# Asking earlier for an expert's first weights, and reordering the first batch's loads, in an attention and mixture-of-experts kernel

## The chip, the cores and the metric

The kernel runs on one core of a Trainium2 chip. The metric is the device time in microseconds (us) of one execution; the median of several runs counts.

## The reference

Sliding-window attention (window 128, a linear bias per head) is followed by a dense mixture of experts. All eight experts work on all tokens; a routing matrix, balanced by eight rounds of row and column normalisation, weighs their outputs.

```python
# q, k, v: (8 batches, 8 heads, 576, 64)
scores = q @ k.T / sqrt(64) + slope[h] * -abs(i - j)   # where 0 <= i - j < 128
attn = softmax(scores) @ v
x = attn.transpose(0, 2, 1, 3).reshape(4608, 512)
P = exp(x @ w_gate - max)
for _ in range(8):
    P /= P.sum(1) + 1e-9; P /= P.sum(0) + 1e-9; P *= N / E
out = sum(P[:, e:e+1] * (relu(x @ w1[e]) @ w2[e]) for e in range(8))   # w1: 512 x 1024, w2: 1024 x 512
```

## The kernel before

**Attention.** Each batch's 576 tokens are four blocks of 128 and a tail of 64. A step of the main loop is (b, kb, u): batch, key block, half of the heads (four). It makes the scores on PE (`scores`, tile psS), their exp on ACT (`exps`, tile pt), the mask product on DVE (`masks`), the product with v on PE (`values`, tile psN), and on DVE the reciprocal and the scaled result xsb. `turn_x` transposes a finished block into xT, the layout that the experts need. Scores, exp and mask of the next step are issued ahead of the values of this one.

**Loads of q and k.** For batch 0 they come in eight pieces on SP's DMA queue (`load_first`, L364), in pairs j = 0 to 3; ACT and DVE cast them to half precision (`cast_qk`), PE turns them (`turn_pe`, tile psT), ACT and DVE copy them to kN and qN. The 64 tail rows of q and k come in one tile t (`load_tail`, L290). They are turned on PE in one piece (`turn_pe` with j = 4), placed ahead of the values of block 2, and copied by ACT to tT; the scores of blocks 3 and 4 read tT. The v blocks (`load_v`, L410) are cast to half precision on POOL (`cast_v`, L423). Tiles of v and t share five buffers (tag s32), so the fifth load of v waits for the cast of the first.

**Weights.** `load_weights` asks for W1 (L100) and W2 (L102) of an expert. These are DMAs of POOL's queue, because they cast from 32 to 16 bits. Their place in POOL's program is the moment of the request: before, W1 of expert 0 stands behind the cast of v0 and ahead of the cast of v1; W2 stands behind two casts of the second half of batch 1's q (L315), which wait for its load (L301).

**The experts in the gaps.** Experts 0 and 1 run during the attention. A `Filler` holds units (expert, first block, number of blocks). A unit has layer-1 pieces (four matmuls into psh, then a relu by ACT or DVE into hT) and layer-2 pieces (matmuls hT by W2 into psy). `take` issues one piece. A unit may start when its blocks are below `filler.ready`. Layer-2 pieces are held back up to step 12 (`filler.hold`). The first two units are (expert 0, blocks 0 and 1) and (expert 0, blocks 2 and 3), with eight layer-1 pieces each, four matmuls of 256 columns per piece.

**Spins.** In the first 42 us PE also runs matmuls on a constant tile (`spin`, `spin_alone`), whose results nobody reads: three ahead of each half-block's values of batch 0, and some alone.

**Order.** The schedule is manual: each engine runs its instructions in the order in which the program issues them, and waits by semaphores. SP's DMAs use eight semaphores in turn, so each waits for the landing of the one eight before. The mask's columns for the tail are made by POOL in `tail_masks`, from columns that ACT's exps (`make_mask`) have written.

Behind the attention come the balancing, and experts 2 to 7 with Strassen's seven products in groups of 256 tokens (L983, L1080); they take some 650 us and the change does not touch them.

Of the kernel before, what the change touches and what calls it, by code (L numbers as in the profile page):

```python
# [9 lines left out]
FP16 = mybir.dt.float16  # L10
# [4 lines left out]
def kernel(  # L15
# [236 lines left out]
    if True:  # L252
# [4 lines left out]
        def make_mask(ys):  # L257
            for y in ys:
                nc.scalar.activation(
                    out=mask[:, y, P : 3 * P], in_=rel, func=AF.Exp, scale=-float(slopes[head_of[y]])  # L260
                )

        def tail_masks():

            nc.gpsimd.memset(mask[TL:P, :, 0:TL], 0.0)
            nc.gpsimd.tensor_copy(out=mask[0:TL, :, 0:TL], in_=mask[0:TL, :, P : P + TL])
            nc.gpsimd.tensor_copy(out=mask[:, :, TL:P], in_=mask[:, :, 2 * P : 2 * P + TL])

# [18 lines left out]
        def load_tail(b):  # L287
            t32 = asb.tile([P, H, Dh], FP32, name=f"t32_{b}", tag="s32", bufs=5)
            for lo, src in ((0, q), (TL, k)):
                nc.sync.dma_start(  # L290
                    out=t32[lo : lo + TL], in_=src[b, :, SM:S, :].rearrange("h s d -> s h d")
                )
            tails[b] = t32

        def load_qk(b, parts=1):
            q32 = per.tile([P, H, RI * Dh], FP32, name=f"q32_{b}", tag="a8", bufs=8)
            k32 = per.tile([P, H, RI * Dh], FP32, name=f"k32_{b}", tag="a8", bufs=8)
            w = H // parts
            for n in range(parts):
                for t, src in ((q32, q), (k32, k)):  # L300
                    nc.sync.dma_start(  # L301
                        out=t[:, n * w : n * w + w],
                        in_=src[b, n * w : n * w + w, 0:SM, :].rearrange("h (p i) d -> p h (i d)", i=RI),
                    )
            raw[b] = (q32, k32)
# [52 lines left out]
        def load_first():  # L358
            q32 = per.tile([P, H, RI * Dh], FP32, name="q32_0", tag="a8", bufs=8)
            k32 = per.tile([P, H, RI * Dh], FP32, name="k32_0", tag="a8", bufs=8)  # L360
            raw[0] = (q32, k32)
            for j in range(NDT):
                for n in (1, 0):
                    nc.sync.dma_start(  # L364
                        out=raw[0][n][:, 2 * j : 2 * j + 2, :],
                        in_=(q, k)[n][0, 2 * j : 2 * j + 2, 0:SM, :].rearrange(
                            "h (p i) d -> p h (i d)", i=RI
                        ),
                    )
            load_v(0)  # L370
            load_v(1)
            load_tail(0)
            load_v(2)
            load_v(3)
            load_v(4)
            homes(0)

        def turn_pe(b, kq, j):
# [27 lines left out]
        def load_v(m):  # L406
            b, kb = divmod(m, NKB)
            v32 = asb.tile([P, H, Dh], FP32, name=f"v32_{b}_{kb}", tag="s32", bufs=5)
            nk = P if kb < NKB - 1 else TL
            nc.sync.dma_start(  # L410
                out=v32[0:nk],
                in_=v[b, :, P * kb : P * kb + nk, :].rearrange("h s d -> s h d"),
            )
            v32s[b, kb] = v32

        def cast_v(m):
            b, kb = divmod(m, NKB)
            vt = asb.tile([P, H, Dh + 2], FP16, name=f"v_{b}_{kb}", tag="v", bufs=6)
            nk = P if kb < NKB - 1 else TL
            if nk < P:  # L420
                nc.gpsimd.memset(vt[nk:P], 0.0)
            nc.gpsimd.memset(vt[0:nk, :, Dh : Dh + 2], 1.0)
            nc.gpsimd.tensor_copy(out=vt[0:nk, :, 0:Dh], in_=v32s.pop((b, kb))[0:nk])  # L423
            vs[b, kb] = vt
# [35 lines left out]
        def exps(b, kb, u):  # L460
            ps = pss.pop((b, kb, u))
            pt = asb.tile([P, 4, 2 * P], FP16, name=f"pt_{b}_{kb}_{u}", tag="pt", bufs=4)
            nc.scalar.activation(out=pt, in_=ps.rearrange("p a y n -> p (a y) n"), func=AF.Exp, scale=scale)  # L463
            pts[b, kb, u] = pt
# [7 lines left out]
        def values(b, kb, u):  # L472

            nk = sizes(kb)
            if u == 0:
                xsbs[b, kb] = asb.tile([P, H, Dh], FP16, name=f"xsb_{b}_{kb}", tag="xsb", bufs=XSB)
            psN = aps.tile([P, GT], FP32, name=f"psN_{b}_{kb}_{u}", tag="pmm", bufs=4)
            if b == 0:
                spin(psN, 3)
            psN = psN[:, 0 : 4 * Dh + 4].rearrange("p (h d) -> p h d", h=4)  # L480
            ops = []
            for y in range(2):
                for hb in range(2):
                    hh = 2 * y + hb
                    if kb > 0:
                        t, at = (pts[b, kb - 1, u], P) if kb < NKB - 1 else (pts[b, kb - 1, u], TL)
                        ops.append((hh, t[:, 2 * hb + y, at : at + P], vs[b, kb - 1][:, 4 * u + hh, 0 : Dh + 1]))
                    t, at = (pts[b, kb, u], P * (kb == NKB - 2)) if kb < NKB - 1 else (pts[b, kb - 1, u], 0)
                    ops.append((hh, t[:, 2 * hb + y, at : at + P], vs[b, kb][:, 4 * u + hh, 0 : Dh + 1]))
            for i, (hh, lhsT, rhs) in enumerate(ops):  # L490
                nc.tensor.matmul(  # L491
                    out=psN[:, hh, :],
                    lhsT=lhsT,
                    rhs=rhs,
                    start=(i == 0),
                    stop=(i == len(ops) - 1),
                )
            if kb > 0:
                pts.pop((b, kb - 1, u))
            rden = asb.tile([P, 4], FP32, name=f"rden_{b}_{kb}_{u}", tag="rden", bufs=2)  # L500
            nc.vector.reciprocal(out=rden[0:nk, :], in_=psN[0:nk, :, Dh])
            nc.vector.tensor_tensor(
                out=xsbs[b, kb][0:nk, 4 * u : 4 * u + 4, :],
                in0=psN[0:nk, :, 0:Dh],
                in1=rden[0:nk, :].unsqueeze(2).to_broadcast([nk, 4, Dh]),
                op=ALU.mult,
            )
# [172 lines left out]
        load_first()  # L680
        spin_alone(20)
        make_mask(range(4))
        load_qk(1, 2)
        load_v(NKB)
        load_tail(1)
        cast_v(0)
        load_weights(0, 0, 1)
        cast_v(1)


        steps = [(b, kb, u) for b in range(B) for kb in range(NKB) for u in range(2)]
        for j in range(2):
            cast_qk(0, j)
            make_mask((4 + 2 * j, 5 + 2 * j))
            if j:
                spin_alone(4)
            turn_pe(0, 1, j)
            turn_pe(0, 0, j)
        tail_masks()
        cast_v(2)  # L700
        nc.gpsimd.dma_start(out=wg_sb, in_=moe_w_gate.rearrange("(dt p) e -> p dt e", p=P))
        cast_v(3)
# [2 lines left out]
            cast_qk(1, j, (0,), True)  # L705
        load_weights(0, 1, 2)
        cast_qk(0, 2)
        cast_qk(0, 3)
        spin_alone(4)
        scores(*steps[0])  # L710
        exps(*steps[0])
        spin_alone(4)
        turn_pe(0, 1, 2)
        turn_pe(0, 0, 2)
# [3 lines left out]
        for n, (b, kb, u) in enumerate(steps):  # L718
# [6 lines left out]
            if nxt:  # L725
                if nxt[0] < XPE and nxt[1:] == (RI - 2, 1):
                    turn_pe(nxt[0], 0, NDT)
                if nxt == (1, 0, 0):
                    filler.ready = RI
                    spin_alone(6)  # L730
                    for _ in range(NFT):
                        filler.take()
                    cast_qk(1, 0)
                    cast_qk(1, 1)
                    for j in range(NDT):
                        turn_pe(1, 1, j)
                        turn_pe(1, 0, j)
                        if j < 2:
                            cast_qk(1, j + 2, (1,))
                        filler.take()  # L740
                if nxt == (2, 0, 0):
                    filler.fill(8.5)
                    cast_qk(2, 0)
                    cast_qk(2, 1)
                    filler.fill(2.5)
                    for j in range(NDT):
                        turn_pe(2, 1, j)
                        turn_pe(2, 0, j)
                        if j < 2:
                            cast_qk(2, j + 2, (1,))  # L750
                        filler.fill(1.0)
                if n == 0:
                    scores(*nxt)
                elif nxt[2] == 0 and nxt[1] < NKB - 1:
                    scores(*nxt)
                    scores(*nxt[:2], 1)
                if nxt[1] < NKB - 1:
                    exps(*nxt)
            if nxt and nxt[1] < NKB - 1:
                masks(*nxt)  # L760
            got = filler.fill(1.0) if b else 0.0
            if (b, kb, u) == (1, 1, 0):
                spin_alone(8)
            values(b, kb, u)
# [572 lines left out]
```

## Time and profile before

| What | Value |
|---|---|
| runs shown | 990.17 us median of 3 (990.02 to 992.47) |
| the profiled execution | 995.15 us, its span 993.3 us |
| PE busy | 978.8 us (99%) |
| DVE, ACT, POOL busy | 692.2, 625.8, 210.5 us |
| PE busy, 0 to 10 us, 10 to 20, 20 to 30 | 6.07, 8.43, 8.61 us |
| PE busy, 30 to 40, 40 to 50, 50 to 60 | 9.17, 8.73, 9.90 us |
| W1 of expert 0 asked for, landed | 13.07, 25.15 us |
| W2 of expert 0 asked for, landed | 31.51, 43.20 us |
| first layer-1 and first layer-2 matmul on PE | 27.28, 43.25 us |

All times within the execution are from the start of its span. Parts of the page that matter here: the busy shares, the queues (q1 is the queue of SP's DMAs, q0 that of POOL's) and the chain that ended last. A landing is the moment at which a DMA's semaphore has its full count.

### The profile page before, as it was taken

Reading aid. Unit: us, or ns where it says so; the run is one execution under the profiler, and the core shown is the slowest. Engines: PE = TensorE matmul, PEld = TensorE weight load, DVE = VectorE, ACT = ScalarE, POOL = GpSimd, SP = SyncE. Lnnn points to the kernel's source line nnn. Section 1 sums busy time; section 2 is a strip of 40 time slices with the busy share of each in tenths; the row PEclk is TensorE's granted clock in tenths of the full one; section 3 lists DMA queues with packets and bytes.
Section 4 is the critical chain, followed back from the end, with each engine's and each line's share of the span. In section 5 each row is a group of like instructions: output and inputs, shape, how many; then the busy total and the mean of one; then the engine's idle time right before and its main releaser. Section 6 shows DMA issues by size and latency. Waiting matters only on the chain.

```text
span 993.3 us, 19600 instructions
## 1 busy us (share of the span) xinstructions
PE 978.8 (99%) x7247; PEld 627.0 (63%) x7247; DVE 692.2 (70%) x1546; ACT 625.8 (63%) x1000; POOL 210.5 (21%) x442
## 2 busy tenths in 40 slices
PE   7999999999999999999999999999999999999998
PEld 5655655565544566666666666666666666666665
DVE  5746766665588878767767676676676676676666
ACT  6645454555343657676776776777677676776774
POOL 3315353545110011111111111111211111111111
PEclk9999999999999999999999999999999999999999
DMA  9998999999999576656667656757756666665666
GB/s 212 237 262 191 211 228 220 221 193 181 229 195 188 92 134 137 128 123 133 129 123 133 146 119 130 147 120 125 144 117 123 143 128 124 141 131 124 142 116 124
DMA packets 383455, 155.03 MB, mean 156 GB/s; under 512 B 335296, under 2 KB 372928, under 8 KB 383360
## 3 DMA queue, kind: packets, MB, share of 16 engines
q1 hardware_dynamic: 359680, 110.87, 56.1%
q0 software_dynamic: 23248, 42.75, 19.8%
q8 instruction: 57, 0.93, 0.4%
q14 instruction: 38, 0.31, 0.1%
q10 hardware_dynamic: 432, 0.16, 0.1%
HBM read 77.25 MB, written 23.59 MB: 102 GB/s over the span
## 4 chain that ended last, share of the span: by engine, by line
PE 90%; DMA 5%; DVE 2%; SPq 1%; issue 1%; ACT 0%; POOL 0%; DVEq 0%; POOLq 0%
PE psM L1080 32%; PE psB L983 14%; PE psy L159 11%; PE psA L983 9%; PE psC L983 9%; PE psh L137 8%; PE psh L118 3%; DMA q<-in_q_dram 1%; PE psN L491 1%; PE psS L457 1%; DMA w2t<-in_moe_w_dram 1%; DMA ysp<-yo 1%; DMA v<-in_v_dram 1%; DMA hs<-s5y 0%; DVE pt L468 0%
## 5 line engine op out<-in xcount | busy, mean ns | idle before, releaser
L1080 PEld LDWEIGHTS <-hs 128*128 128x128 f16 x2996 | 292.6, 98 | 122.7 <-DVE hs L1051 0.8
L983 PEld LDWEIGHTS <-xset 128*128 128x128 f16 x1484 | 144.9, 98 | 91.2 <-issue 0.9
L1051 DVE TENSOR_TENSOR hs<-hs 128x512 f16<-128x512 f16 x535 | 194.3, 418 | 10.1 <-DMA hs<-hr 8.1
L1080 PE MATMUL psM<-w2l,hs 128*128 128x256 f16 x1440 | 195.3, 273 | 0.3 <-DVE hs L1051 0.3
L159 PE MATMUL psy<-w2t,hT 128*128 128x512 f16 x576 | 135.7, 379 | 0.8 <-DMA w2t<-in_moe_w_dram 0.8
L1021 ACT ACTIVATE hr<-hr,L_sb 128x512 f16<-128x512 f16 x142 | 98.5, 716 | 53.7 <-DVE hr L1035 51.4
L1080 PE MATMUL psM<-more,hs 128*128 128x256 f16 x864 | 121.0, 273 | 0.0
L1035 DVE TENSOR_TENSOR hr<-psB,s5y 128x512 f16<-128x512 f32 x71 | 49.0, 691 | 89.6 <-PE psB L983 88.8
L983 PE MATMUL psB<-s,xset 128*128 128x512 f16 x356 | 105.7, 378 | 0.2 <-ACT psB L1211 0.2
L983 PE MATMUL psA<-w1l,xset 128*128 128x512 f16 x356 | 105.9, 379 | 0.0
L149 ACT ACTIVATE hT<-psh 128x512 f16<-128x512 f32 (+1 forms) x104 | 60.4, 581 | 70.0 <-PE psh L137 69.9
L137 PE MATMUL psh<-xT,w1t 128*128 128x512 f16 (+1 forms) x448 | 99.0, 364 | 0.1
L463 ACT ACTIVATE pt<-psS 128x1024 f16<-128x1024 f32 x64 | 64.6, 1022 | 51.0 <-PE psS L457 50.5
L159 PEld LDWEIGHTS <-hT 128*128 128x128 f16 x576 | 54.1, 98 | 59.7 <-DMA w2t<-in_moe_w_dram 1.1
L1215 ACT COPY psC<-psB 128x512 f32<-128x512 f32 x106 | 60.4, 570 | 48.5 <-PE psB L983 48.0
L1139 POOL COPY held_at<-hr 128x2 f16<-128x2 f16 x54 | 10.1, 187 | 341.6 <-ACT hr L1021 341.5
L582 DVE CAST yo<-psy 128x512 f16<-128x512 f32 x65 | 44.5, 689 | 51.0 <-PE psy L159 48.3
L1124 DVE TENSOR_TENSOR acc<-acc,psM 128x256 f32<-128x256 f32 (+1 forms) x162 | 77.0, 503 | 2.7
L1211 ACT COPY psB<-psA 128x512 f32<-128x512 f32 x106 | 60.4, 570 | 25.3 <-PE psA L983 22.6
L468 DVE TENSOR_TENSOR pt<-pt,mask 128x1024 f16<-128x1024 f16 x64 | 53.1, 830 | 30.8 <-ACT pt L463 30.8
L1213 ACT COPY s5y<-psC 128x512 f32<-128x512 f32 x106 | 62.8, 592 | 7.0 <-PE psC L983 7.0
L137 PEld LDWEIGHTS <-w1t 128*128 128x128 f16 x448 | 41.3, 98 | 37.7 <-issue 0.8
(145 smaller groups left out, 1351.4 us busy)
## 6 DMA issues: line engine op xcount, KB each, us to landing
ysp<-yo SPq DMA_DIRECT2D x65, 128.0 KB, 3.9
v<-in_v_dram SPq DMA_DIRECT2D x32, 256.0 KB, 4.1
out_dram<-acc POOLq DMA_DIRECT2D x30, 256.0 KB, 2.6
q<-in_q_dram SPq DMA_DIRECT2D x5, 1024.0 KB, 7.0
k<-in_k_dram SPq DMA_DIRECT2D x5, 1024.0 KB, 9.6
y_e<-ysp POOLq DMA_DIRECT2D x36, 128.0 KB, 2.4
consts<-ysp POOLq DMA_DIRECT2D x36, 128.0 KB, 2.6
consts<-xd POOLq DMA_DIRECT2D x34, 128.0 KB, 2.4
```

The source lines that it names most:

```text
L137: nc.tensor.matmul(out=ps[:, 0:nt], lhsT=w1ts[e][:, dt, P * ft : P * ft + P], rhs=xT[:, at : at + nb, dt, :], start=(dt == 0), stop=(dt == ...
L149: nc.scalar.activation(out=st["hT"][:, ft, 0:nt], in_=ps[:, 0:nt], func=AF.Relu)
L159: nc.tensor.matmul(out=ps, lhsT=st["hT"][:, ft, P * ms : P * ms + P], rhs=w2ts[e][:, ft, :], start=(ft == 0), stop=(ft == NFT - 1),)
L463: nc.scalar.activation(out=pt, in_=ps.rearrange("p a y n -> p (a y) n"), func=AF.Exp, scale=scale)
L983: nc.tensor.matmul(out=psum(name), lhsT=xset[n // NE % 2][:, x, P * k : P * k + P], rhs=q[k], start=(start and k == 0), stop=(k == 1), ski ...
L1021: nc.scalar.activation(out=quarter(n, slot), in_=src, func=AF.Relu, scale=P_sb[:, blk, e : e + 1])
L1051: nc.vector.tensor_tensor(out=t[:, AT.get(to, to)], in0=t[:, AT[x]], in1=t[:, AT[y]], op=op)
L1080: nc.tensor.matmul(out=ps, lhsT=hs[n % 2][:, LEFT[m], f, :], rhs=W2L[e][RIGHT[m]][:, f, :], start=(e == 2 and f == 0 and half == 0), stop= ...
L1124: nc.vector.tensor_tensor(out=a, in0=a, in1=p2, op=op)
L1211: nc.scalar.copy(out=psum("B"), in_=psum("A"))
L1213: nc.scalar.copy(out=s5, in_=psum("C"))
L1215: nc.scalar.copy(out=psum("C"), in_=psum("B"))
```

## The change

1. W1 of expert 0 is asked for behind a new instruction on POOL, a copy of two columns of qN of j = 1 into a new tile `w1_gate`. The copy's result is not used; it makes POOL wait until DVE has written that piece of qN. The request stands ahead of the cast of v0, and the mask's tail columns (a memset and two copies) ahead of both.
2. On SP's queue, v2 and v3 of batch 0 go ahead of the two tail loads, and v4 follows them. `load_qk(1, 2)`, `load_v(NKB)`, `load_tail(1)` keep their places behind v4. On POOL the casts of v keep their order.
3. The ACT cast of k's fourth piece (j = 3) goes behind the first exp.
4. In the last block of batch 0 (kb = 4), two layer-1 pieces are issued ahead of each half-block's values, the first two in units that may start once two blocks are ready. The three spins ahead of these values, twice, and six spins ahead of the eight layer-1 pieces that follow are removed. The units have as many pieces as before, so four pieces leave their later places in the first half-blocks of batch 1.

In the built program PE has 12 matmuls fewer, POOL one copy more; other engines have the same instructions.

```diff
+        w1_gate = asb.tile([P, 2], FP16, name="w1_gate")
         def tail_masks():
-            nc.gpsimd.memset(mask[TL:P, :, 0:TL], 0.0)
...
             load_v(0)
             load_v(1)
-            load_tail(0)
             load_v(2)
             load_v(3)
-            load_v(4)
+            load_tail(0)
...
-            if b == 0:
+            if b == 0 and kb < NKB - 1:
                 spin(psN, 3)
...
         make_mask(range(4))
-        load_qk(1, 2)
-        load_v(NKB)
-        load_tail(1)
-        cast_v(0)
-        load_weights(0, 0, 1)
-        cast_v(1)
...
+        nc.gpsimd.memset(mask[TL:P, :, 0:TL], 0.0)
         tail_masks()
+        nc.gpsimd.tensor_copy(out=w1_gate, in_=QKT[0][0][:, 1, 0:2])
+        load_weights(0, 0, 1)
+        cast_v(0)
+        load_v(4)
+        load_qk(1, 2)
+        load_v(NKB)
+        load_tail(1)
+        cast_v(1)
         cast_v(2)
...
         cast_qk(0, 2)
-        cast_qk(0, 3)
         spin_alone(4)
         scores(*steps[0])
         exps(*steps[0])
+        cast_qk(0, 3)
...
                     filler.ready = RI
-                    spin_alone(6)
                     for _ in range(NFT):
                         filler.take()
...
             got = filler.fill(1.0) if b else 0.0
+            if b == 0 and kb == NKB - 1:
+                filler.ready = 2
+                for _ in range(2):
+                    filler.take()
```

## The prediction

> **What bounds the kernel now.** I read the busy shares of the windows first, then the chain of waits over the first 46 us, then the DMA queues in short windows, and last the timelines of PE, POOL, ACT, DVE and SP up to 55 us. The windows view has, per stretch, its length, the busy time of PE, PEld, DVE, ACT and POOL, then granted clock, DMA share and GB/s.
>
> ```profile
> 7.70:11.11 3.41, 1.69 (x16) 1.13 (x17) 1.46 (x3) 0.94 (x3) 0.00 (x0) 1.00 1.05 279
> 11.11:14.52 3.41, 3.02 (x24) 2.25 (x23) 2.53 (x4) 2.69 (x5) 2.00 (x4) 0.50 0.58 131
> ...
> 43.25:54.85 11.60, 11.26 (x136) 6.66 (x137) 8.66 (x23) 3.60 (x5) 5.24 (x12) 1.00 1.04 254
> 54.85:993.30 938.45, 933.01 (x6720) 594.72 (x6718) 656.42 (x1461) 591.76 (x944) 193.06 (x401) 1.00 0.75 152
> ```
>
> From 54.85 on PE is busy 933 of 938 us at full clock, and before that it is not. On PE nothing is removed or moved behind 40, so the change is worth exactly what it moves the start of this dense part. What sets that start is in the chain (start, length, what):
>
> ```profile
> 12.52 0.61 POOL v L423
> 13.13 0.83 POOL w1t L100
> ...
> 16.39 13.88 DMA q<-in_q_dram
> ...
> 30.39 1.11 POOL c L315 x2
> 31.51 11.70 DMA w2t<-in_moe_w_dram
> 43.20 0.05 issue
> 43.25 1.04 PE psy L159 x4
> ```
>
> The first layer-2 product waits for W2 of expert 0. POOL asks for W2 at 31.51, behind two casts of batch 1's q, which landed at 30.27. PE had reached that product at 42.45 and idled 0.80 us. By then all 16 layer-1 pieces of the first two units were done (8 from 27.28, 4 between the turns of batch 1, 4 from 36.80 and 38.99). So: **the end is max(PE's arrival, W2's landing), plus a fixed rest.** Arrival is 42.45, landing 43.20.
>
> **Removed spins and moved pieces.** Twelve spin matmuls go: six at 26.63, three each at 25.48 and 36.22. Six took 26.63 to 27.28, 0.108 each: 1.3 us. In their place at 25.48 come two layer-1 pieces (8 matmuls, 36.80 to 37.66, 0.87 us); two more go ahead of the values at 36.56. No piece is new: the four leave 36.80 and 38.99, where they stood beside PE's wait for the masks (psN at 37.86 starts when DVE's mask of 37.11 to 37.80 is done). So arrival gains little by itself: -0.65 (six spins), +0.55 (0.87 for 0.32), -0.40 (the wait for v4's cast at 26.20 goes, if v4 is in), and 0 to -0.9 around batch 1's first half-blocks, of which I take -0.3, since psX at 41.12 waits for an xsb that comes that much sooner. Sum -0.8, arrival at 41.6. By itself this is worth nothing: it only lengthens the wait for W2.
>
> **W1 earlier.** POOL now runs the mask's tail first (0.52 + 0.76 + 0.60 us; ACT's last mask exp ends at 7.5, so by 8.9), then the gate, which waits for DVE's qN copy of j=1 (9.73 + 0.69 = 10.42). The gate's own copy has no row here; the same 128x2 copy at L1139 takes 0.19 on average, so 0.1 to 0.2. W1 is asked for at about 10.65 instead of 13.07, 2.4 us sooner. Behind it on POOL wait v0's cast (landing 12.47, so covered) and the rest of the casts. The mask copies no longer run beside DVE's masks (the mask at 16.50 took 1.14 against 0.69): -0.45 there, lost again in the next wait. The cast of k's fourth part behind the first exp costs nothing: qN of j=3 (13.10), which the next scores wait for, waits for q's last part (landed 11.77).
>
> **What W1 does to SP's queue** is the large term. These are the queues in four windows (packets, MB, share): 14 to 15.7 before W1's first packet, 16.6 to 18.5 and 18.5 to 22 during W1, 36 to 40 during W2.
>
> ```profile
> q1 hardware_dynamic: 1716, 0.43, 116.6%
> ...
> q0 software_dynamic: 122, 0.25, 84.0%
> ...
> q0 software_dynamic: 286, 0.59, 94.0%
> q1 hardware_dynamic: 231, 0.06, 12.8%
> ...
> q0 software_dynamic: 598, 0.61, 92.2%
> q1 hardware_dynamic: 524, 0.13, 25.6%
> ```
>
> Alone, SP's queue (q1) moves 1,000 of v's 256-byte packets per us. Once W1's packets come (q0, 2.7 us after the request) it stands still for 2 us, and then gets about one packet per W1 packet, 66 to 130 per us. The view of the v loads says the same in landing times: issued at 12.3 and 13.0 they took 4.0 us, issued at 13.7, behind W1's request, 11.8:
>
> ```profile
> DMA to landing us min/median/max: 3.9/4.0/4.0
> ...
> DMA to landing us min/median/max: 11.8/11.8/11.8
> ```
>
> In the changed kernel W1's packets come at about 13.3. By then the profile has 2,650 small packets moved from 8.2 on, which is v0, v1 and half of v2. Half of v2 (512), v3 (1,024), both tails (1,024) and v4 (512) are still behind, where before only v4 was. v2 mostly slips through, as v3 did (landed 17.02, 1.3 us after W1's first packet). v3 and the tails do not. The nearest row is W2's: landed at 43.20, 11.69 after its request, with the v load stuck behind it at 43.53 and the next 1,024 packets at 44.31, 1.11 after W2. W1 took 12.08 from its request, so it lands at 10.65 + 12.08 = 22.7, v3 at 23.1 and **the tails at 23.8**. Bounds: 22.0, if only W1's bulk counts (its first 432 of 512 packets went from 15.7 to 22.0, so up to 19.6 now): of the 2,560 packets ahead some 400 slip through and 85 per us follow for 4 us, and the 1,800 left run at 1,000 per us and land 0.6 later. 24.6, if the tails come like the last transfer stuck behind W2, which landed at 45.05, 1.85 after it.
>
> Before, the tails landed at 15.07 and PE turned them at 19.59:
>
> ```profile
> 19.59 0.63 PE L387 MATMUL psT<-consts,t 128*128 128x128 f32 x4
> ...
> 26.20 0.37 PE L491 MATMUL psN<-v,pt 128*128 128x65 f16 x7 [0.20 <-POOL v L423]
> ```
>
> PE takes its matmuls in order, so values of block 2, the scores of block 3 (they read tT) and everything behind stand until 23.9: 4.3 us later. Nothing takes that up: from 19.59 to 25.48 the old timeline is one chain (turn, ACT's tT at 20.26, exps of 1.03 at 20.74, 22.22 and 23.13, mask, values). With the -0.65 + 0.55 - 0.40 above, layer 1 starts at 27.28 + 4.3 - 0.5 = 31.1, and PE arrives at 42.45 + 3.8 - 0.3 = 46.0. W2 is not what is late then: q's second half stands behind the same transfers as before, so W2 lands at 43.2 or up to 1 us sooner. The dense part starts 46.0 - 43.25 = 2.7 us later.
>
> **Clock.** The 3.41 us window with PE busy 1.69 was followed by one at granted clock 0.50. The stall leaves about 1.5 busy in 17.94 to 21.35 and 0.8 in the next, so PE works at half clock up to 28.2. In the old window at 0.50 sixteen turns took 1.98 us, against 0.45 for eight warm: 1.1 us more. Part lies beside ACT's exps: 0 to 1.3, I take 0.6. The Trainium skill (TensorE: Matmul & The Clock Gate, section on what's actually happening) has the clock halved only after a wholly idle window of about 3.4 us. By that rule only the stretch from 24.8 is cold, and the sum would be 0.2 lower; the trace speaks against it, since 7.70 to 11.11 was half busy.
>
> **Sum.** +2.7 + 0.6 = **+3.3 us**. The profiled execution took 995.15 (span 993.3) and would take 998.4; the median shown is 990.17, so **993.5**. The forecast's own ends: tails at 22.0, no price for the clock and the full -0.9 give 46.0 - 1.8 - 0.6 - 43.25 = +0.4; tails at 24.6, 1.3 for the clock and 0 in place of the -0.3 give 2.7 + 0.8 + 1.3 + 0.3 = +5.1. So 990.6 to 995.3. A measurement of this kernel can tell about 0.3% (3 us) from no change.
>
> **Rivals.**
> - *The tails come in time* (not slower). If W1's transfer is short or lets SP's queue run, the tails land by 19.6. For it: SP's ring was already filled with v3 when W1 came before. Against it: three stuck v loads. Then arrival is about 41.6 and W2's landing decides, 42.2 to 43.2: -1.0 to 0, so **989.9**. It decides where the tails land before about 20.5 (46.0 + 0.6 less 3.3 is 43.3). The Trainium skill (DMA: Bandwidth & Descriptors, anatomy of the SWDGE path) fits a GpSimd transfer at 2.0 us plus bytes over 436 GB/s, an estimate of 4.4 us for W1; by that the tails would be in time and this rival would hold. The trace has 12.08 and 11.69.
> - *W2 comes forward with W1* (faster). If all of W1's 2.4 us pass on to q's second half, W2 lands at 40.8 and PE, at 41.6 to 40.5 with every unsure term taken, decides; up to 1 us of the waits between 43.25 and 54.85 can go too: 986.7 to 988.5, taken **988.2**. Against it: the DMA engines are full from 14 us on, so order changes and the sum does not.
> - *The gate or the exp's new place delays the first scores*: at 13.13 to 14.25, priced 0 to 0.5; inside the ranges.
>
> **Chances.** Forecast 0.68, of which 0.48 lies over the 0.3% bound and 0.20 under it; tails in time 0.19; W2 forward 0.13, 0.08 of it beyond the bound. So faster 0.08, same 0.20 + 0.19 + 0.05 = 0.44, slower 0.48. The range 988.5 to 995.5 takes in the forecast's and the first rival's ends and leaves out W2's case below 988.5, about 0.1.
>
> **What would show it.** Right: W1 asked for near 10.7; v3 and tails over 8 us from issue to landing; an idle PE of 3 to 5 us ahead of psT from t; half clock after 21 us; no wait at the first psy. Wrong: psT from t at 19 to 20 us, or a longer wait of psy for w2t. If PE's dense part does not start later than before, the tail step failed; if it starts later without a wait for t, my size of the others did.

## The result, and the profile after

| | before | after |
|---|---|---|
| median | 990.68 us (6 runs, 990.02 to 992.47) | 996.26 us (6 runs, 995.69 to 996.75) |
| ratio, 95% interval | | 1.0049 [1.0035, 1.0062] |
| profiled execution, span | 995.15, 993.3 us | 996.75, 994.6 us |
| W1 asked for, landed (us from the span's start, as below) | 13.07, 25.15 | 9.08, 19.51 |
| tails (k's part) landed, turned by PE | 15.07, 19.59 | 22.19, 22.28 |
| first layer-1, first layer-2 matmul | 27.28, 43.25 | 28.92, 45.76 |
| W2 landed | 43.20 | 40.40 |

The changed kernel is 5.6 us slower; 3.3 were forecast, and 996.26 lies above the range's 995.5. In the windows view of the changed kernel (columns as in the prediction) the same stretches answer to those of before: a window in which PE does nothing, one at half clock, and the dense part.

```profile
18.76:22.18 3.42, 0.00 (x0) 0.00 (x0) 0.31 (x1) 0.00 (x0) 2.38 (x5) 1.00 1.02 215
22.18:25.59 3.41, 3.31 (x41) 2.90 (x43) 0.64 (x2) 2.19 (x4) 0.85 (x3) 0.50 1.25 321
...
54.85:994.65 939.80, 934.98 (x6742) 596.15 (x6739) 656.45 (x1468) 591.95 (x944) 197.44 (x401) 1.00 0.72 151
```

The chain of waits (start, length, what) says what PE waited for. It runs through SP's issue of the v loads, then of the tails, and through the k tail's 7.04 us to the turn on PE:

```profile
7.54 2.36 SPq L410
...
9.94 1.05 SPq L410
...
11.03 4.08 SPq L291
...
15.15 7.04 DMA t<-in_k_dram
22.19 0.09 issue
22.28 1.09 PE psT L387 x4
...
45.28 0.54 PE psS L457 x8
45.83 0.32 PE psy L159
```

Before, this chain ended with DMA w2t. Now W2 is no link of it: it landed at 40.40, and 5.4 us later PE came. The PE timeline shows the wait itself, and a turn at half clock (1.09 us for the four transposes against 0.63):

```profile
22.28 1.09 PE L387 MATMUL psT<-consts,t 128*128 128x128 f32 x4 [4.82 <-DMA t<-in_k_dram]
```

The DMA queues in the windows 9.7 to 11.7, 11.7 to 14 and 14 to 17.5 us (packets, MB, share) show why the tails are late. SP's queue (q1) moves 816 packets per us while W1's first packets (q0) come in, and from 14 on one for each of W1's, 92 per us:

```profile
q1 hardware_dynamic: 1632, 0.41, 121.5%
q0 software_dynamic: 9, 0.02, 6.7%
...
q0 software_dynamic: 180, 0.37, 88.7%
q1 hardware_dynamic: 332, 0.08, 24.2%
...
q0 software_dynamic: 311, 0.63, 94.6%
q1 hardware_dynamic: 322, 0.08, 17.4%
```

A turn of q0 carries 2 KB and one of q1 256 bytes, so v2, v3 and the tails wait until W1 has gone through. v2 and v3, asked for at 7.54 and 9.94, both took this long:

```profile
DMA to landing us min/median/max: 11.1/11.1/11.1
```

### The profile page after: what moved, and what is told of

Same layout as the page of the kernel before. It is cut to its first block, busy times and chain, and to the rows that moved or that the text cites. A ratio compares the mean times of both kernels' runs of the same rounds, so it can differ in the third digit from the quotient of the medians.

```text
span 994.6 us, 19577 instructions
## 1 busy us (share of the span) xinstructions
PE 977.7 (98%) x7235; PEld 626.7 (63%) x7235; DVE 689.5 (69%) x1546; ACT 626.0 (63%) x1000; POOL 214.5 (22%) x443
## 4 chain that ended last, share of the span: by engine, by line
PE 94%; DMA 2%; SPq 1%; DVE 1%; ACT 1%; issue 0%; POOL 0%; DVEq 0%; ACTq 0%
PE psM L1084 32%; PE psB L987 14%; PE psy L159 12%; PE psA L987 9%; PE psC L987 9%; PE psh L137 9%; PE psh L118 4%; PE psN L491 2%; PE psS L457 1%; DMA t<-in_k_dram 1%; SPq L410 1%; DVE pt L468 1%; DMA out_dram<-acc 0%; DMA hs<-hr 0%; PE psT L387 0%; DMA hs<-s5y 0%
```

## The experiments

Theory: what SP still has in its queue when W1's packets come waits until W1's bulk is over; in the changed kernel that takes in the tails, and PE, which runs in order, stands ahead of transposing them ("turned" in the tables). "The product" is the first layer-2 product. Rivals are named run by run. The landing, turn and product times come from the one profiled execution of each run, the medians from all of its executions. Ratios are to the kernel before on the same chip. Its medians there were 991.63 us (e1 to e4), 992.59 (e5 to e8) and 991.71 (e9 to e11).

**e1 and e10: the kernel before, unchanged.**

> The kernel before, once more, to have a second profiled execution of it. Theory (the startup of the execution shown before was some 4 us longer than that of the other runs, 995.15 against 990.7): the time is 990.7, and this profile has its first psy near 39 us instead of 43.25, with k and q pieces that land earlier (q's second piece at 7 instead of 8.8). Rival (the 4.5 us lie in the dense part or outside the span): first psy again near 43.

> The kernel before once more, for a third profile. Two profiles of it have the first layer-2 product at 43.25 and at 39.82. Theory (the profile shown with the prediction was a late start: the second piece of q landed at 8.78 instead of 6.81, and a half clock followed): 39.5 to 41, no window at half clock in the first 30 us, psT from the tails at 17 to 17.7. Rival (the two are equally usual): near 43 again.

e1: 992.60 us, 1.0010 [0.9996, 1.0023]; e10, one execution, 989.67. In both profiles q's second piece landed at 6.8 (8.78 in the profile shown with the prediction), no window of the first 30 us had half clock, the tails were turned at 17.08 and 17.19, and the first layer-2 product came at 39.82 and 39.83, not at 43.25. This is e10's PE timeline:

```profile
17.19 0.63 PE L387 MATMUL psT<-consts,t 128*128 128x128 f32 x4
...
39.83 1.04 PE L159 MATMUL psy<-w2t,hT 128*128 128x512 f16 x4
```

W2 landed at 39.53 and 39.46, just ahead of PE, and PE's waits name no weight. The chain of e10 has its last transfer, k's fourth piece, before 9.1 us; from there to the product it is ACT, DVE and PE alone:

```profile
3.87 5.23 DMA k<-in_k_dram
9.12 0.62 ACT c L319
...
38.59 0.44 DVE xsb L502
39.02 0.05 issue
39.07 0.29 PE psX L530 x2
39.35 0.54 PE psS L457 x8
39.90 0.97 PE psy L159 x4
```

So in these executions no transfer bounds the start, and a weight that lands sooner has nothing to give. Both are short executions of their kernel, though: 990.26 is the lowest of e1's twelve, and 989.67 lies below all fifteen of the kernel before on that chip (from 990.22). The start of one like the median may come a little later; no profile shows it.

**e11: the changed kernel again.**

> The changed kernel once more, for a second profile. Theory: PE waits 4 to 5.5 us for the tails, turns them at 22 to 23.5, a half-clock window follows, the first layer-2 product comes at 45.3 to 46.5 and does not wait for W2. Rival (the first profile was as late a start as that of before): tails at 20 to 21, the product at 43 to 44.

One execution, 997.40 us. PE waited 4.55 us for the tails, turned them at 21.99, and the product came at 44.69 (0.6 sooner than expected), with W2 landed at 41.28. Two profiles of each kernel now stand apart by 4.9 to 5.9 us at this product, and the medians by 5.6. The agreement is a rough one, since short executions of the kernel before stand here beside long ones of the changed kernel (996.75 is the highest of its six).

**e2, e3, e4: one part undone at a time.** e2 puts the tails back ahead of v2; e3 puts W1 back behind v0's cast; e4 is the kernel before with the spins removed and the pieces moved.

```diff
 e2 (against the changed kernel)
             load_v(1)
+            load_tail(0)
             load_v(2)
             load_v(3)
-            load_tail(0)
 e3 (against the changed kernel)
-        nc.gpsimd.tensor_copy(out=w1_gate, in_=QKT[0][0][:, 1, 0:2])
-        load_weights(0, 0, 1)
         cast_v(0)
+        load_weights(0, 0, 1)
```

> The changed kernel with the tail loads again ahead of v2 and v3. Theory (W1's early transfer starves whatever stands behind it on SP's queue, whichever load that is): the tails land by 14, PE's wait of 4.8 us for t goes, and a wait of about 4 us for the casts of v2 and v3 takes its place, since v2 now lands near 21 and v3 near 22: 995 to 996, first psy within 1 us of the 45.8 of the changed kernel. Rival (the order of the loads is the cause): the wait goes, 991 to 992, first psy at 41 to 42.

> The changed kernel with W1 asked for behind the cast of v0 again; its order of v and tails, its pieces and its spins are kept. Theory: W1's packets come at about 14.8 instead of 11.7, v3 has landed by then and the tails are at most partly stuck; no wait for t over 1.5 us; 990 to 991.5. Rival (pieces and spins cost the time, by the clock or by late values): 994 to 996.

> The kernel before with the third part of the change alone: two layer-1 pieces ahead of each half-block's values of block 4, twelve spins fewer. Theory: PE arrives earlier at W2's wait and waits longer, 990.0 to 990.7. Rival (PE's arrival sets the end in a usual execution, W2 does not): up to 1.3 us faster, 989.4 to 990.0.

| | W1 asked | k tail asked, landed | turned | product | median, ratio |
|---|---|---|---|---|---|
| e4: tails first, W1 late | 12.05 | 10.10, 14.16 | 17.42 | 40.84 | 990.92, 0.9996 [0.9984, 1.0008] |
| e2: tails first, W1 early | 8.99 | 9.57, 19.41 | 19.55 | 42.71 | 994.33, 1.0027 [1.0014, 1.0039] |
| e3: v first, W1 late | 11.88 | 12.23, 22.32 | 22.41 | 45.85 | 995.50, 1.0037 [1.0023, 1.0051] |
| after: v first, W1 early | 9.08 | 15.15, 22.19 | 22.28 | 45.76 | 996.26, 1.0049 [1.0035, 1.0062] |

The pieces and spins cost nothing that can be measured (e4). In e4's profile the product waited 0.96 us for W2 (landed 40.79), so W2 is not out of the way in every execution; e6 and e9 try it.

For e2 and e3 the expectations of the theory were missed. For e2 I had both tails in by 14, the wait moved to v's casts and 995 to 996 us: q's tail was in at 13.22, but k's was still behind W1's packets, so most of the wait stayed with the tails (2.38 us, against 0.63 for a cast of v), and the product came 3 us sooner than expected. For e3 the miss was 4 us: I had taken W1's earlier request for the cause, and the order of the loads brings most of the loss without it. (e3 keeps the moved cast and mask copies too, but PE stood ready for the tails at 17.34, hardly later than e10's turn at 17.19.) The reason is the same meeting: in e3 the k tail is asked for 0.35 us after W1 and is stuck, as in e2, where it is asked for 0.58 us after. The PE timelines of e3 and of e2 show the wait with the same releaser:

```profile
22.41 1.09 PE L385 MATMUL psT<-consts,t 128*128 128x128 f32 x4 [5.07 <-DMA t<-in_k_dram]
```

```profile
19.55 0.63 PE L387 MATMUL psT<-consts,t 128*128 128x128 f32 x4 [2.38 <-DMA t<-in_k_dram]
```

So either edit puts the k tail behind W1. Both together cost little more than the order alone (1.0049 against 1.0037), and W1's earlier request alone about half of it (1.0027). What separates e4 from the rest is that its tails are in, at 14.16, when W1's packets come: none had by 14.05, and two by 14.25. To be asked for first is not enough: v2 of the changed kernel was asked for 1.5 us ahead of W1 and took 11.1 us.

**e5: v first, and W1 only once the tails are in.**

```diff
-        nc.gpsimd.tensor_copy(out=w1_gate, in_=QKT[0][0][:, 1, 0:2])
-        load_weights(0, 0, 1)
         cast_v(0)
...
         cast_v(1)
+        nc.gpsimd.tensor_copy(out=w1_gate, in_=tails[0][:, 0, 0:2])
+        load_weights(0, 0, 1)
```

> The changed kernel with the order v2, v3, tails on SP's queue kept, and W1 of expert 0 asked for on POOL behind a copy that reads the tail tile, so only once both tails have landed. The earlier looks show that v2 and v3 ahead of the tails cost 4.6 us even with W1 behind v0's cast, because W1's packets start before the tails' turn has come. Theory (only the meeting of W1's packets with the tails on SP's queue costs; the order as such is free): tails land at 14 to 15.5, PE turns them at 17 to 17.5 with no wait over 0.5 us, W1 is asked for at 15 to 16 and lands near 26, layer 1 starts at 26 instead of 23.4 to 24.6 without moving the first layer-2 product by more than 1 us; time 990.5 to 992.5. Rival (the order v2, v3, tails costs by itself, or W1 must not come later than about 22): the tail turn is on time but layer 1 or the first layer-2 product is 2 to 3 us late, 993 to 995.

999.21 us, 1.0070 [1.0054, 1.0085]: above both forecasts, and against the change's 1.0049 the intervals overlap. (The profiled execution, 1001.32, is one of the longest of the six.) The first half of the theory held: tails in at 16.45, turned at 17.68 without a wait. But W1, asked for at 16.86, landed at 28.98, and layer 1 waited for it. The PE waits of e5 and its windows:

```profile
PE psh L137 <- DMA w1t<-in_moe_w_dram: 4.8, 1, 4.8
```

```profile
21.03:24.44 3.41, 1.96 (x29) 1.22 (x25) 2.92 (x8) 1.89 (x3) 1.88 (x4) 1.00 1.11 248
24.44:27.86 3.42, 0.00 (x0) 0.00 (x0) 0.42 (x1) 0.00 (x0) 0.73 (x2) 0.50 1.14 209
27.86:31.27 3.41, 2.24 (x18) 1.75 (x19) 0.32 (x1) 0.39 (x1) 0.00 (x0) 0.50 1.35 187
31.27:34.68 3.41, 3.41 (x21) 2.54 (x19) 1.12 (x4) 1.27 (x3) 0.67 (x2) 0.50 1.22 197
```

The wait is again 4.8 us long, at another place, and PE is at half clock from 24.44 to 34.68. The product came at 48.18, 8.4 us later than in e10: 4.8 of them are this wait, and the other 3.5, with half clock in most of that stretch, no run here takes apart. W1 has a due time of its own, about 24, when PE began to stand. The order of the kernel before keeps both: in e4 the tails were in 3.3 us before their turn, and W1 landed at 22.51, 0.9 us before layer 1 began. That W1 could be asked for 4 us later at no price was my error.

**e7: half of W1 at the early place, the other half behind the tails.**

```diff
-        load_weights(0, 0, 1)
+        load_w1_half(0)          # rows 0 to 255
         cast_v(0)
...
         cast_v(1)
+        t_gate = asb.tile([P, 2], FP16, name="t_gate")
+        nc.gpsimd.tensor_copy(out=t_gate, in_=tails[0][:, 0, 0:2])
+        load_w1_half(1)          # rows 256 to 511
```

> The changed kernel with W1 of expert 0 asked for in two requests: rows 0 to 255 at the place of the change, rows 256 to 511 on POOL behind a copy that reads the tail tile. Half the packets and half the bytes stand in front of the tails. Theory (SP's queue stands for as long as W1's packets last): half as long a stand, about 3 to 3.5 us less, so the tails land at 18 to 19 and PE waits 0.5 to 1.5 us before it turns them; the second half lands near 27, in time for layer 1 or 1 us late; 991.5 to 993.5. Rival (each request stops SP's queue for a fixed time, or the second request stops what follows as much again): PE's wait before the tails stays above 3.5 us, or the same wait appears at v3 or at batch 1's turns, 995 to 997.

996.35 us, 1.0042 [1.0027, 1.0057]. From W1's first request (10.24) to the k tail's landing (19.50) it takes 9.3 us, against 13.1 in the changed kernel: with half of W1's packets ahead of them the tails come 3.9 us sooner, as the theory said. The wait for the tails is only 0.63 us, in part because this execution started late: q's second piece landed at 8.08, a window at half clock followed, and PE reached the tails at 18.96, not 17.46. The time was lost elsewhere, and came out in the rival's 995 to 997. The second half of W1 cost 1.9 us as the rival said (landed 28.46), again with half clock behind it. Another 0.9 us is the edit's own: v2 had landed at 16.89, but its cast stands on POOL behind the copy that waits for the tails, and ran at 20.77.

**e8: the wait filled with 36 spins.**

```diff
                 if nxt[0] < XPE and nxt[1:] == (RI - 2, 1):
+                    if nxt[0] == 0:
+                        spin_alone(36)
                     turn_pe(nxt[0], 0, NDT)
```

> The changed kernel with 36 matmuls on the constant tile ahead of the turn of batch 0's tails on PE, 3.9 us of work nobody reads, which lies inside the 4.8 us wait for the tails. Theory (the wait costs its length, and the half clock behind it only some tenths more): no window at half clock after 20 us, the tail turn still at 22.3, the distance from the tail turn to the first layer-2 product falls from 23.5 to 22.8 us; 0.3 to 0.9 faster than the changed kernel, 995.3 to 996. Rival (the half clock carries 1.5 us or more of the loss): 994 to 995.

997.28 us, 1.0045 [1.0032, 1.0058], above both forecasts; the interval holds the change's ratio, so the time does not separate the theories, and the profile does. In e8's windows the half clock is gone:

```profile
17.84:21.25 3.41, 3.41 (x33) 2.94 (x30) 1.18 (x3) 0.00 (x0) 1.18 (x2) 1.00 0.98 204
21.25:24.66 3.41, 1.89 (x33) 1.54 (x32) 0.00 (x0) 1.31 (x2) 2.03 (x6) 1.00 1.09 294
```

From the tail turn (22.68) to the product (45.30) it takes 22.62 us, against 23.48 in the profile after, so in this pair the half clock is worth 0.86 us. In e11, also with a window at half clock, it takes 22.70, and in e10 22.64. So behind the turn at most 0.9 us are lost, and the rest of the loss is the wait's own length.

**e6 and e9: can W2 come sooner?** Both are e4 with W2 asked for behind the first half of batch 1's k; e9 also loads the second v block of batch 1 ahead of batch 1's tails.

```diff
+        w2_gate = asb.tile([P, 2], FP16, name="w2_gate")
+        nc.gpsimd.tensor_copy(out=w2_gate, in_=raw[1][1][:, 0, 0:2])
+        load_weights(0, 1, 2)
         for j in (2, 3):
             cast_qk(1, j, (0,), True)
-        load_weights(0, 1, 2)
 e9 in addition
         load_v(NKB)
+        load_v(NKB + 1)
         load_tail(1)
...
-                if n // 2 + NKB + 1 < B * NKB:
+                if 1 < n and n // 2 + NKB + 1 < B * NKB:
                     load_v(n // 2 + NKB + 1)
```

> The kernel before with the spins removed and the four layer-1 pieces moved up, and W2 of expert 0 asked for on POOL behind a copy that reads the first half of batch 1's k, ahead of the two casts of the second half of q. In the run with the pieces alone, PE reached the first layer-2 product at 39.88 and waited 0.96 us for W2, landed 40.79 after a request at 28.92. Theory (W2's landing is a bound that sits 0 to 1 us behind PE when nothing else is late): W2 is asked for near 26.5 and lands near 38.3; the second half of q is issued long before and its packets are through by 29, that of k loses up to 1 us; PE reaches the product at 39.9 without a wait: 0.5 to 1 us faster than the pieces alone, 989.5 to 990.5. Rival (W2's earlier packets hold back the second half of k and the v load behind it, as W1's do to the tails): the turns of batch 1 wait 2 us or more, 992 to 994.

> The run with W2 asked for 1.3 us sooner (27.66), and in addition the v load of batch 1's second block ahead of batch 1's tail loads on SP's queue. In that run no wait for W2 was left, but the v load stood behind it, landed at 39.50, and PE waited 1.56 us for its cast. Theory (queue order alone: what is asked for ahead of the weight's packets goes through, what is asked for behind them waits until the bulk is over): the v load lands before 33, the wait ahead of the values at 40 is gone, the tails of batch 1 land near 40 instead, which nobody needs before 43.5; the first layer-2 product starts at 39.5 to 40.3; 0.5 to 1.2 us faster than the kernel before. Rival (the DMA engines are full up to W2's landing, so the wait turns up at the next load in the queue, the tails or the first half of batch 2's q): a new wait of 1 us or more within 50 us and the same time as before.

e6: 992.17 us, 0.9998 [0.9989, 1.0006], so the forecast gain of 0.5 to 1 us does not show. W2 was asked for 1.3 us sooner than in e4 and nothing waited for it, but a v load asked for 1.1 us behind it was stuck, and PE waited 1.56 us for its cast. In the chain of e6:

```profile
28.79 10.71 DMA v<-in_v_dram
39.50 0.05 issue
39.55 0.61 POOL v L423
40.16 0.06 POOL v L422
40.23 0.36 PE psN L491 x7
```

e9: 991.86 us, 1.0003 [0.9993, 1.0013]. That v load landed at 31.04, batch 1's tails took its place (37.06 and 37.98) with nobody waiting, and the product came at 39.68 without a wait, as expected. The 0.5 to 1.2 us were missed: the time stayed that of before, whose short executions have the product at 39.8 as well. Behind it e9's rest took 951.2 us, against 948.0 in e10. No version beat the kernel before by more than the measurement can tell.

## Why the prediction was wrong in size

**The step that failed** is the base of the last subtraction: "The dense part starts 46.0 - 43.25 = 2.7 us later", and with it "The profiled execution took 995.15 (span 993.3) and would take 998.4; the median shown is 990.17, so 993.5". 43.25 belongs to a late start of that one execution: a piece of q at 8.78, PE idle for 1.96 us, a window at half clock, W2 at 43.20. Why that piece was late is open. The other two profiles have 39.8, so the distance is 4.9 to 5.9 us, and the medians' 5.6 fits it. I took the 5.0 us between that execution and the median to be common to both kernels. But 3.4 us lay in the very stretch that I subtracted, which the profiles e1 and e10 do not have; they are also 1.5 to 2.1 us shorter behind the product. With 39.8 in place of 43.25 my other terms give 46.0 + 0.6 - 39.8 = 6.8 us, somewhat more than the 5.6 measured. The signs were there: 995.15 was above all three runs shown, and the half clock was in the window that I quoted.

Point by point:

- **Bound.** "max(PE's arrival, W2's landing), plus a fixed rest" described that execution; in e1 and e10 W2 is in 0.3 to 0.4 us ahead of PE, in e4 0.96 us behind it. The rest behind the product is not quite fixed: 947.8 to 951.2 us over the thirteen profiles, for which I have no cause.
- **Spins and pieces**, worth nothing by themselves: right (e4). The 0.8 us by which PE was to arrive sooner are less: from the tail turn to PE's arrival at the product e4 takes 22.46 and e9 22.31, e10 22.64 and e1 22.74.
- **W1 earlier.** The gate's copy took 0.31, not 0.1 to 0.2. Asked for at 9.08 instead of 10.65, because qN came sooner; landed after 10.4 us instead of 12.08. All of W1's gain stood idle: layer 1 started 9.4 us after its landing.
- **SP's queue.** Mechanism right, place right. Alone it moved 816 packets per us, not 1,000. v2 did not slip through (11.1 us), and the k tail landed 2.7 us behind W1 (2.0 in e11), not 1.1. The later landing after W1 and the earlier W1 cancel in part: tails at 22.2 for a forecast of 23.8, and PE's wait 4.8 and 4.6 us for 4.3. That these came so near is partly luck, since both the early W1 and PE's earlier readiness go with a start that was not late.
- **PE and W2.** Forecast "PE arrives at 46.0" and 0.6 for the clock; measured 45.76 and 44.69, without a wait for W2: right, and the price of the wait is its length (e8).
- **Clock.** 0.86 us in e8's comparison for a forecast of 0.6; that is one pair of profiles, and against e11 it would be 0.1. The prediction's aside was inconsistent: by its own 1.5 and 0.8 us busy no window would be wholly idle, so the rule that it quotes would make none cold, and the sum would have been 0.6 lower, not 0.2. In the run the window was empty. One window at half clock, up to 25.59 instead of 28.2; in e3, where the wait sat differently in the windows, two.
- **Rivals.** Tails in time: excluded by the 4.82 us. W2 forward with W1: it landed sooner (40.40) and was not what decided. The gate: no wait of it in PE's list. The exp's new place: PE waited 0.63 us at 10.72 for the cast of k's fourth piece that now stands behind the exp, a little over the 0 to 0.5 priced; at the values ahead of the tail turn only 0.1 us of it is left (17.06, against 16.95 in e10).

## What to carry to other kernels

Ahead of a large transfer on another queue, list what the small-packet queue will still hold when its packets come, and give each of these loads its due time; a 128 KB load asked for 0.4 us behind W1 took 10.1 us (e3), the same load asked for 2 us ahead of it 4.1 (e4). What counts is what has landed when the first packets come, 2.0 to 2.4 us behind the request in e4 and in the changed kernel. Before a wait in one profile is taken as the bound, hold the profiled execution's time against the other runs: where it lies above all of them, part of its waits may be its own (here 3.4 us), and the distance should be taken to an execution like the median's. A weight's landing is worth moving only if the engine that uses it waits for it there.

## What the runs showed of the hardware

**Turns of the queues.** From 14 to 17.5 us 311 packets of W1 and 322 of SP's queue went through. The Trainium skill (DMA: Bandwidth & Descriptors, section Queues, rings and completion order) has each DMA engine take turns between queue rows packet by packet; the trace agrees with turns of one for one if the profile's packet is the unit; whether it is, no run here shows.

**Half clock after part-idle windows.** Windows with PE busy for 0.98 (e2), 1.46 and 1.77 (e7), 1.69 (before) and 1.96 us (e5) of 3.41 were each followed by one at 0.50; 1.85 (e6), 1.89 (e8), 1.91 (e7) and 2.28 (e3) were not. So the busy time of a window does not decide it alone. Once at half clock, 2.24 (e5) and 2.36 us (e3) did not lift it, and 3.02 (before) to 3.41 did. The Trainium skill (TensorE: Matmul & The Clock Gate, section What's actually happening) has the clock fall after an idle window; the empty windows here agree, and it does not cover those five part-busy ones. That nothing less than an idle window does it was the prediction's reading of it.
